# The second MLP product of a two-layer transformer kernel with seven block products instead of eight, on one Trainium2 core

## The chip, the core and the metric

The kernel runs on one core of a Trainium2 chip. A core has engines that run side by side, each with an instruction queue of its own: TensorE (PE in the profile; PEld are its weight loads), VectorE (DVE), ScalarE (ACT), GpSimd (POOL) and SyncE (SP), which here only issues DMA transfers. Transfers are issued from SP's queue and from ScalarE's (SPq and ACTq in the profile). Each engine takes its instructions in the order in which the program lists them, and an instruction waits on semaphores for those of other engines. TensorE multiplies from SBUF (128 partitions) into PSUM (eight banks of 2 KB a partition); the others read and clear PSUM. The metric is the time of one execution in microseconds, as the median of several runs.

## The reference

```python
def _A_ref(x, wqkv, wo):              # H = 32 heads of Dh = 20, window W = 256
    qkv = (x @ wqkv).reshape(B, S, 3, H, Dh).transpose(2, 0, 3, 1, 4)
    q, k, v = qkv[0], qkv[1], qkv[2]
    scores = jnp.einsum("bhqd,bhkd->bhqk", q, k) * (Dh ** -0.5)
    mask = (idx[:, None] - idx[None, :] >= 0) & (idx[:, None] - idx[None, :] < W)
    p = _softmax(jnp.where(mask[None, None], scores, -1e9))
    return jnp.einsum("bhqk,bhkd->bhqd", p, v).transpose(0, 2, 1, 3).reshape(B, S, D) @ wo

def _B_ref(x, w1, b1, w2, b2):        # D = 640, F = 1536
    h = jnp.einsum("bsd,df->bsf", x, w1) + b1
    r = jnp.where(h > 0, h, 0)
    return jnp.einsum("bsf,fd->bsd", r * r, w2) + b2

for _ in range(2):                    # x: 1 x 2048 x 640, the same weights in both layers
    x = x + _A_ref(_layernorm(x), wqkv, wo)
    x = x + _B_ref(_layernorm(x), w1, b1, w2, b2)
```

## The kernel before

**Numbers.** All is float32 in memory. Each large product is done with float16 halves: a matrix is split into a high part and the rest (low), and `mm3` (L256) issues three matmuls for each chunk of 128 rows of the contraction: high by high, high by low, low by high. The weights are converted once, at the start: `convert` (L196) writes the high half on ScalarE (L198) and the low half on VectorE (L199), and wq_s, wo_s, w1_s and w2_s then stay in SBUF for both layers. Weights on their way in are staged in memory that is free at that time: `load_wo` and `load_w1` stage in w2_s (L192), and `load_w2` in `krow[2]`, the memory of a later group's keys.

**Groups.** The 2048 tokens are worked through in 8 groups of T = 256, twice (two layers), so 16 units u. A unit's own attention runs beside the dense work of its neighbours, which stands in Python generators that yield after about 0.5 us of matmuls: `stage_qk(u + 1)` and `stage_v(u + 1)` (queries, keys and values of the next group), `stage_o(u - 1)` (output projection), `y_cross` (the second layernorm's result, transposed by DMA), and `stage_f(u - 1)` (the MLP). `together` (L930) deals these out between the eight quads of heads of the unit's attention. A quad is `max_quad` (scores for the row maxima: matmuls L548, VectorE L560), for every second quad `max_out` (transposes the maxima, L573, and puts them into the queries as two more rows by DMA), `exp_quad` (scores again, now less the maxima: matmuls L611, exponentials on ScalarE L624, and masks on GpSimd L639 and L643), and `pv_quad` (the values: float32 matmuls L673, which wait for the masks; ScalarE copies them out, L685). The output projection reads the values back through memory, transposed and divided by the sums of the exponentials (`load_o`; reciprocals L749).

**PSUM.** Two tiles of three banks hold scores (`banks`, name bb); the two banks that are left go in turn to all dense products, values and transposes (`mm_tile`, tag "mm").

**Order.** The program writes out the order of every engine's queue itself. Work for ScalarE ("A"), VectorE ("D"), GpSimd ("G") and DMA issue ("S") is posted as a Job with a cost in ns, a priority and the jobs that it depends on; a small clock for each engine (`pump`, `step`) places them as TensorE's planned time goes by, and `need` moves the planned time to the end of a job. So the order of a queue follows planned times, but on the chip each instruction just waits for its semaphores, in that order. FCST, CARRY and KEEP (L964) are planned costs of stages, by which `together` spreads the dense work.

**The MLP.** `stage_f` (L829) first does the first product, six times two chunks f of 128 hidden columns, 15 matmuls of 256 columns each: ScalarE adds b1 and takes relu (L844, out of PSUM into a float32 tile r), GpSimd squares (L848), ScalarE copies to the high half (L851), VectorE subtracts for the low half (L854), both into the tile hh. Then `ln_cross` posts the layernorm and the DMA transposes of the group after next. The second product takes two halves i of the tokens by two halves h of the 640 columns: 36 matmuls of 320 columns over 12 chunks, weights hh (loaded into TensorE), moving w2_s. VectorE adds each to the residual x1 (L881), to which GpSimd has added b2 (`add_b2`, L803), and x1 is stored (L890). The memory of hh (tag "hh") is also used by `stage_qk`, `y_cross` (through `beside`) and `load_o`.

## Time and profile before

| | before |
|---|---|
| median of 3 runs | 1628.66 us (1627.52 to 1630.12) |
| the profiled execution's span | 1624.5 us; the profile gives no time beside it |
| instructions in the span | 44743 |
| TensorE: idle before matmuls of the first MLP product | 4.5 us in the whole span |
| TensorE: idle before matmuls of the second MLP product | 0.0 us |
| mean rate of memory traffic | 85 GB/s read and written |

The profile is of one execution. Its page gives, for each engine, the busy time and its share of the span. The chain of waits follows the work that ended last back from the end: each row is a start, a length, an engine, and an instruction by its line with what it writes and reads. The instructions in order of time have the same columns for all work, with runs of equal instructions as one row (x35). A row of groups has busy time and mean ns of one behind the first bar, and the idle time of the engine just before these instructions, with what ended it, behind the second; "[7.81 <-ACT r L844]" is the same for one row. A row of a stretch has the length, then for PE, PEld, DVE, ACT and POOL the busy time with the count of instructions, then the clock granted to TensorE (1.00 is full), the share of time that the 16 DMA engines were busy, and GB/s. DMA issues have median issue, the range of their starts, and the median time to landing. "spin" are matmuls without use that the kernel issues at the start.

### The profile page before, as it was taken

The page shows a single profiled execution, that of the slowest core. Times are in us where ns is not written, and L with a number is a line of the kernel's source. Part 1 is how long each engine was busy: PE and PEld are TensorE (multiplying, and loading weights), DVE is VectorE, ACT ScalarE, POOL GpSimd, SP SyncE. Part 2 cuts the span into 40 slices and gives each one's busy share as a digit, 9 for nine tenths or more (in the row PEclk, how much of TensorE's full clock was granted, in tenths as well). Part 3 has the DMA queues.
Part 4 walks back from the last instruction along what each step waited for, and adds up shares of the span by engine and source line. Part 5 has one row for each costly group of instructions (what it writes and reads, how often), then busy time and mean ns, then how long its engine had stood idle before and what let it go on. Part 6 is the DMA issues. An engine that isn't in the chain of part 4 may idle for free.

```text
span 1624.5 us, 44743 instructions
## 1 busy us (share of the span) xinstructions
PE 1591.8 (98%) x17686; PEld 1181.1 (73%) x17686; DVE 1043.5 (64%) x3250; ACT 736.4 (45%) x1593; POOL 614.5 (38%) x1288
## 2 busy tenths in 40 slices
PE   8998999999999999999999999999999999999999
PEld 7676767777777777777777777777777777776667
DVE  8776775666756657665556766567675666757441
ACT  4555535444453444545344453534535444454522
POOL 1224524334352443535233352533534334343512
PEclk9999999999999999999999999999999999999999
DMA  9863253351434434343352434334343351431020
GB/s 272 204 173 93 59 127 75 109 113 50 115 83 116 90 73 113 70 119 79 94 132 58 119 77 121 80 94 107 67 115 79 106 112 50 108 75 54 26 65 17
DMA packets 234217, 158.09 MB, mean 97 GB/s; under 512 B 82200, under 2 KB 217752, under 8 KB 234008
## 3 DMA queue, kind: packets, MB, share of 16 engines
q1 hardware_dynamic: 227640, 145.74, 36.6%
q10 hardware_dynamic: 6368, 9.50, 1.9%
q8 instruction: 139, 2.28, 0.6%
q14 instruction: 70, 0.57, 0.1%
HBM read 84.68 MB, written 52.95 MB: 85 GB/s over the span
## 4 chain that ended last, share of the span: by engine, by line
PE 90%; DVE 4%; ACT 3%; DMA 1%; issue 1%; POOL 1%; SPq 0%; DVEq 0%; POOLq 0%; ACTq 0%
PE acc L261 67%; PE pv L673 10%; PE bb L611 6%; PE bb L548 5%; DVE bb L560 2%; ACT pt L624 1%; PE spin L275 1%; PE tr L573 1%; DMA o<-ot 0%; ACT r L844 0%; DMA od<-o 0%; DVE mx L560 0%; ACT qd L435 0%; DVE qd L438 0%; DVE mT L579 0%
## 5 line engine op out<-in xcount | busy, mean ns | idle before, releaser
L560 DVE CUSTOM_DVE_ANT_0 bb<-bb,maskb 128x384 f32<-128x384 f32 (+2 forms) x1024 | 510.6, 565 | 103.6 <-PE bb L548 95.9
L624 ACT ACTIVATE pt<-bb 128x512 f32<-128x512 f32 (+1 forms) x736 | 376.0, 600 | 235.8 <-PE bb L611 229.2
L639 POOL TENSOR_SCALAR_AFFINE_SELECT pt<-pt 128x256 f32<-128x256 f32 x448 | 198.8, 449 | 564.3 <-ACT pt L624 543.9
L261 PE MATMUL acc<-y,w_s 128*128 128x256 f16 x2880 | 330.4, 273 | 4.5 <-DVE y L311 1.4
L261 PE MATMUL acc<-w_s,hh 128*128 128x320 f16 x2304 | 326.7, 300 | 0.0
L261 PEld LDWEIGHTS <-w_s 128*128 128x128 f16 x2880 | 277.5, 98 | 58.0 <-issue 25.8
L261 PEld LDWEIGHTS <-hh 128*128 128x128 f16 x2304 | 222.0, 98 | 98.1 <-issue 15.3
L261 PEld LDWEIGHTS <-wq_s 128*128 128x128 f16 x2400 | 230.6, 98 | 47.0 <-issue 17.5
L261 PE MATMUL acc<-yT,wq_s 128*128 128x256 f16 x2250 | 258.9, 273 | 4.1 <-DMA yT<-yl 1.0
L643 POOL TENSOR_SCALAR_AFFINE_SELECT pt<-pt 128x256 f32<-128x256 f32 x512 | 220.1, 452 | 93.2 <-ACT pt L624 85.6
L854 DVE TENSOR_TENSOR hh<-r,hh 128x256 f16<-128x256 f32 x192 | 91.5, 498 | 204.7 <-ACT hh L851 197.1
L673 PE MATMUL pv<-pt,vt 128*32 128x128 f32 (+1 forms) x3840 | 187.5, 329 | 2.8 <-DVE x L783 1.7
L848 POOL TENSOR_TENSOR r<-r 128x256 f32<-128x256 f32 x192 | 113.8, 614 | 182.1 <-ACT r L844 180.6
L685 ACT COPY ot<-pv 128x256 f32<-128x256 f32 x128 | 47.7, 372 | 283.9 <-PE pv L673 283.8
L560 DVE DVE_READ_ACCUMULATOR2_ANT mx<- 128x1 f32 x1024 | 143.2, 140 | 0.0
L261 PE MATMUL acc<-wo_s,od 128*128 128x320 f16 x960 | 139.6, 301 | 0.0
L673 PEld LDWEIGHTS pv<-pt,vt 128*32 128x32 f32 x3840 | 104.0, 109 | 48.6 <-issue 18.2
L261 PE MATMUL acc<-wq_s,yT 128*128 128x320 f16 x900 | 132.2, 299 | 3.6 <-DVE y L311 1.9
L844 ACT ACTIVATE r<-acc,b1s 128x256 f32<-128x256 f32 x192 | 80.7, 472 | 98.5 <-PE acc L261 97.0
L261 PEld LDWEIGHTS <-od 128*128 128x128 f16 x960 | 92.0, 98 | 43.4 <-issue 8.7
L261 PEld LDWEIGHTS <-yT 128*128 128x128 f16 x900 | 86.6, 98 | 41.2 <-issue 10.7
L611 PE MATMUL bb<-qt,kt 62*128 62x128 f16 (+1 forms) x1920 | 107.1, 244 | 4.1 <-DVE mx L560 3.0
(82 smaller groups left out, 1182.7 us busy)
## 6 DMA issues: line engine op xcount, KB each, us to landing
qt<-qk SPq DMA_DIRECT2D x30, 480.0 KB
kt<-qk SPq DMA_DIRECT2D x30, 480.0 KB
qk<-qd SPq DMA_DIRECT2D x17, 640.0 KB
o<-ot SPq DMA_DIRECT2D x256, 42.0 KB
od<-o SPq DMA_DIRECT2D x14, 640.0 KB
qk<-yl SPq DMA_DIRECT2D x13, 640.0 KB
qk<-qd SPq DMA_DIRECT2D x17, 320.0 KB
xt<-in_A_x_dram SPq DMA_DIRECT2D x16, 320.0 KB
```

What stands on the lines that cost most here:

```text
L261: nc.tensor.matmul(acc, lhs(a, c), rhs(b, c), start=(k == 0), stop=(k == 3 * nk - 1))
L548: nc.tensor.matmul(to, qt[r, p, i * P:(i + 1) * P], kt[r, p, a:b], start=True, stop=True)
L560: nc.vector.tensor_tensor_reduce(out=v, in0=v, in1=mask, scale=1.0, scalar=-3.0e38, op0=ALU.add, op1=ALU.max, accum_out=accum),
L611: nc.tensor.matmul(bb[e][:, k, o:o + w], kt[r, 2 * qd + j, ko:ko + P], qt[r, 2 * qd + j, q0 * P:q0 * P + w], start=True, stop=True)
L624: nc.scalar.activation(box["pt"][:, :o], bb[e][:, k, :o], AF.Exp, scale=SCALE / (QS * QS))
L639: nc.gpsimd.affine_select(out=m, in_=m, pattern=[[0, 2], [-1, P]], compare_op=ALU.is_gt, fill=0.0, base=0, channel_multiplier=1)
L643: nc.gpsimd.affine_select(out=m, in_=m, pattern=[[0, 2], [1, P]], compare_op=ALU.is_ge, fill=0.0, base=0, channel_multiplier=-1)
L673: nc.tensor.matmul(pv[32 * jj:32 * (jj + 1), q0 * P:(q0 + qn) * P], vf[:, c:c + 32], pj[:, j, :], start=(k == 0), stop=(k == len(steps) - ...
L685: nc.scalar.copy(ot[:, qd % 2], pv)
L844: nc.scalar.activation(box["r"], acc[:, f, :], AF.Relu, bias=b1s[:, f0 + f:f0 + f + 1], scale=1.0 / (YS * WS))
L848: nc.gpsimd.tensor_tensor(box["r"], box["r"], box["r"], op=ALU.mult)
L854: nc.vector.tensor_sub(hh[:, 1, f, :], box["r"], hh[:, 0, f, :])
```

## The change

The second product Y = A B (A: 256 tokens by 1536 hidden columns, squared; B: w2) is cut once in each of its three dimensions: tokens into halves i, hidden columns into halves k (chunk p goes with chunk p + 6, a pair), columns into halves h. With A11, A12, A21, A22 (first index the token half) and B likewise, Winograd's form of Strassen's method computes seven products of sums instead of eight:

- on the left: A11, A12, S1 = A21 + A22, S2 = S1 - A11, S4 = A12 - S2, S3 = A11 - A21, A22, of which the tile r holds some with the other sign; the weights' signs go with them;
- on the right: the seven matching blocks or sums of blocks of w2;
- the four outputs as sums of the products. Products are numbered j = 0 to 6, and one of them goes into one or two of the outputs x1 (list ADDS).

What it does to the code, with line numbers of the changed kernel where the prediction uses them:

- **First product's evictions** now run by pairs p of chunks, six a group, in a tile r of eight blocks of 128 columns (two such tiles instead of four of 256 columns): per chunk relu on ScalarE and square on GpSimd as before, then on GpSimd three instructions for the sums (128, 256 and 128 columns), one copy of 896 columns to the high half (ScalarE, L937) and one subtraction of 896 columns for the low half (VectorE, L941). The halves go into two tiles (tags "ha" and "hb").
- **Second product**: 7 products x 6 pairs x 3 = 126 matmuls of 320 columns in 21 pieces (two pairs of a product each), in the order PIECES. Products 0, 2, 4 and 5 add up one after the other in one PSUM bank, "x": VectorE reads it after each, and the next starts only after the reads. Products 1, 3 and 6 use the other bank, "y", each by itself. There are eight adds into x1 on VectorE (L993) instead of four. The two banks stay open over several pieces, so `some` and `together` hold back attention's use of the "mm" banks while they are open.
- **Weights**: the sums of w2's blocks are formed at the start on GpSimd, split into halves on ScalarE and VectorE, and written to device memory (w2d, 6 x 1.15 MB), staged through the ring's memory. `fetch` then reads pieces of 327,680 B back into a ring of seven places, from ScalarE's DMA queue, one for every piece of every group (336 in all). Each waits for the matmuls that free its place, and for the fetch eight transfers before it. w2_s is gone; `load_w1` and `load_wo` stage in other memory. The first seven fetches stand behind the first group's attention; group 0's first product waits for the weight sums, since they use the same tiles r.
- **Planned costs**: FCST, CARRY and KEEP are changed.

```diff
+FP = FC // 2
+SLOTS = 7
...
-    w2_s = sb.tile([P, 2, FC, D], F16, name="w2_s")
+    ring = sb.tile([P, SLOTS, 2, 2, HD], F16, name="ring")
+    w2d = tc.dram_tile([P, 7, FC // 2, 2, HD], F16, name="w2d")
...
     def load_w2():
...
+
+        v = w2.rearrange("(k c p) n -> c p k n", p=P, c=FP)
+        places = [hraw2[:, :2 * D], hraw2[:, 2 * D:4 * D], krow[2][:, :2 * D]]
+        outs = [ringraw[:, k * 7 * HD:(k + 1) * 7 * HD].bitcast(F16).rearrange("p (j a n) -> p j a n", a=2, n=HD)
+                for k in range(2)]
+        lows, done = {}, {}
+        for p in range(FP):
+            st, out = places[p % 3], outs[p % 2]
+            free = lows[p - 3] if p > 2 else [[*w1s[1]], [*w1s[2]], [gate2]][p]
+            load = bulk(lambda st=st, p=p: nc.scalar.dma_start(st.rearrange("p (k n) -> p k n", k=2), v[p]),
+                        P * 2 * D * 4, gate, *free)
+            q = st.rearrange("p (k n) -> p k n", n=HD)
+            box = {}
+
+            def sums(box=box, q=q):
+                box["t"] = t = sb.tile([P, 8, P], F32, name="r", tag="r", bufs=2)
+                t = t.rearrange("p a n -> p (a n)")[:, :3 * HD].rearrange("p (a n) -> p a n", n=HD)
+                box["t"] = t
+                nc.gpsimd.tensor_tensor(t[:, 1:3], q[:, 1:2].to_broadcast([P, 2, HD]), q[:, 0::3], op=ALU.subtract)
+
+            def more(box=box, q=q):
+                nc.gpsimd.tensor_tensor(box["t"][:, 0], q[:, 3], box["t"][:, 1], op=ALU.subtract)
+
+            def last(box=box, q=q):
+                t = sb.tile([P, 8, P], F32, name="r", tag="r", bufs=2)
+                box["l"] = t = t.rearrange("p a n -> p (a n)")[:, :HD]
+                nc.gpsimd.tensor_tensor(t, q[:, 2], box["t"][:, 0], op=ALU.subtract)
+
+            j = post("G", 1600, sums, load, *(lows.get(p - 1, ())), prio=2)
+            j = post("G", 850, more, j, prio=2)
+            j = post("G", 850, last, j, prio=2)
+            kinds = [(lambda q=q: q[:, 0::2], slice(0, 2), WS, 2, load), (lambda box=box: box["t"], slice(2, 5), WS, 3, j),
+                     (lambda box=box: box["l"], 5, WS, 1, j), (lambda q=q: q[:, 3], 6, -WS, 1, load)]
+            lows[p] = []
+            for src, at, s, n, d in kinds:
...
+                a = post("A", 60 + 0.85 * n * HD, high, d, *done.get(p - 2, ()), *(w1j.values() if p < 2 else ()), prio=2)
+                lows[p].append(post("D", 60 + 1.1 * n * HD, low, a, prio=2))
+            done[p] = [bulk(lambda out=out, p=p: nc.scalar.dma_start(w2d[:, :, p], out), P * 14 * HD * 2, *lows[p])]
+        w2l.extend(j for k in range(FP) for j in lows[k])
+        w2j.extend(j for k in range(FP) for j in done[k])
...
+    PIECES = [("x", 0, 0), ("x", 0, 1), ("y", 1, 0), ("y", 1, 1), ("x", 0, 2), ("y", 1, 2)] + [
+        (b, j, g) for b, j in (("x", 2), ("y", 3), ("x", 4), ("y", 6), ("x", 5)) for g in range(3)]
+    PLACE = [0, 1, 4, 6, 5, 2, 3]
+    slots = {}
+
+    def fetch(n, *deps):
+
+        _, j, g = PIECES[n % len(PIECES)]
+        if n < len(PIECES) * NU:
+            slots[n] = post("A", 150.0, lambda: nc.scalar.dma_start(ring[:, n % SLOTS], w2d[:, j, 2 * g:2 * g + 2]), *deps,
+                            prio=1, size=P * 4 * HD * 2, land=2200.0)
...
+            sides[u] = sb.tile([P, 2, KC * 2 * T], F16, name="yl", tag="hb", bufs=1)
...
+            raw = sb.tile([P, 2, KC, T], F32, name="od", tag="ha", bufs=1)
...
     def stage_f(u, ahead=None):
...
+        if u == 0:
+            need(*w2l)
+        hs = [sb.tile([P, 2, FP // 2, 7, P], F16, name="hh", tag=t, bufs=1) for t in ("ha", "hb")]
         hj = []
...
+        for p in range(FP):
             acc, jobs = mm_tile([P, 2, T], "acc")
...
+            def evict(wait, acc=acc, jobs=jobs, p=p):
+                box, js = {}, []
+                for k in range(2):
+                    def blocks(box=box, k=k):
+                        return box["r"][:, 1:3] if k else box["r"][:, 0::7]
+
+                    def relu(k=k, acc=acc, box=box, blocks=blocks):
+                        if k == 0:
+                            box["r"] = sb.tile([P, 8, P], F32, name="r", tag="r", bufs=2)
+                        f = p + k * FP
+                        nc.scalar.activation(blocks(), acc[:, k, :].rearrange("p (i n) -> p i n", i=2), AF.Relu,
+                                             bias=b1s[:, f:f + 1], scale=1.0 / (YS * WS))
+
+                    def square(blocks=blocks):
+                        nc.gpsimd.tensor_tensor(blocks(), blocks(), blocks(), op=ALU.mult)
+
+                    j = post("A", 360, relu, *hj[max(p - 2, 0):max(p - 1, 0)], *jobs[-1:], wait=wait, prio=0)
                     jobs.append(j)
...
+                    js.append(post("G", 571, square, j, prio=0))
+
+                def s1(box=box):
+                    r = box["r"]
+                    nc.gpsimd.tensor_tensor(r[:, 6], r[:, 7], r[:, 2], op=ALU.add)
+
+                def s23(box=box):
+                    r = box["r"]
+                    nc.gpsimd.tensor_tensor(r[:, 4:6], r[:, 6:8], r[:, 0:1].to_broadcast([P, 2, P]), op=ALU.subtract)
+
+                def s4(box=box):
+                    r = box["r"]
+                    nc.gpsimd.tensor_tensor(r[:, 3], r[:, 4], r[:, 1], op=ALU.subtract)
+
+                def high(box=box):
+                    nc.scalar.copy(hs[p // 3][:, 0, p % 3], box["r"][:, 0:7])
+
+                def low(box=box):
+                    h = hs[p // 3]
+                    nc.vector.tensor_sub(h[:, 1, p % 3], box["r"][:, 0:7], h[:, 0, p % 3])
+
+                j = post("G", 330, s1, *js, prio=0)
+                j = post("G", 571, s23, j, prio=0)
+                j = post("G", 330, s4, j, prio=0)
+                j = post("A", 830, high, j, prio=0)
+                hj.append(post("D", 1060, low, j, prio=0))
+
+            for k in range(2):
+                fo = (p + k * FP) * P
+                need(w1j[p + k * FP])
+                yield from mm3(acc[:, k, :], lambda a, c: w1_s[:, a, c, fo:fo + P],
+                               lambda b, c: y2[:, b, c, :], KC, 109, evict if k else None)
         if ahead is not None:
             ln_cross(ahead, *b2j)
...
+        x1 = [x1s.pop((u, i)) for i in range(2)]
+        ADDS = [[(0, 0)], [(0, 0)], [(0, 1)], [(1, 1), (0, 1)], [(1, 1)], [(1, 0)], [(0, 1)]]
+        LAST = {1: [(0, 0)], 6: [(0, 1)], 4: [(1, 1)], 5: [(1, 0)]}
+        reads = []
+        started = set()
+        for n, (bank, j, g) in enumerate(PIECES):
+            n += u * len(PIECES)
+            if opened[bank] is None:
                 acc, jobs = mm_tile([P, 2 * T], "acc")
...
+                hold = Job("S", 0.0, None, [], 0.0, 0)
+                jobs.append(hold)
+                opened[bank] = acc, jobs, hold
+                started.discard(bank)
+            acc, jobs, hold = opened[bank]
+            if bank == "x" and g == 0 and reads:
+                need(*reads)
+            need(slots[n])
+            for c in range(2):
+                p = 2 * g + c
+                need(hj[p])
+                for k, (a, b) in enumerate(((0, 0), (0, 1), (1, 0))):
+                    nc.tensor.matmul(acc[:, :HD], hs[p // 3][:, a, p % 3, PLACE[j], :], ring[:, n % SLOTS, c, b, :],
+                                     start=bank not in started, stop=(p == FP - 1 and k == 2), skip_group_check=True)
+                    started.add(bank)
+                if c == 0:
+                    yield 408
+            used_ = Job("S", 0.0, None, [], 0.0, 0)
+            used_.end = now[0] + 408
+            fetch(n + SLOTS, used_)
+            if g < 2:
+                yield 408
+                continue
+            js = []
+            for i, h in ADDS[j]:
+                hs_ = slice(h * HD, (h + 1) * HD)
+
+                def add(x=x1[i], acc=acc, hs_=hs_):
+                    nc.vector.scalar_tensor_tensor(x[:, hs_], acc[:, :HD], 1.0 / WS, x[:, hs_], op0=ALU.mult, op1=ALU.add)
+
+                js.append(post("D", 408, add, *b2j[2 * i + h:2 * i + h + 1], wait=408, prio=0))
+            jobs.extend(js)
+            if bank == "x":
+                reads = js
+            if bank == "y" or j == 5:
+                jobs.remove(hold)
+                opened[bank] = None
+            for i, h in LAST.get(j, ()):
+                b, hs_ = 2 * g_(u) + i, slice(h * HD, (h + 1) * HD)
                 if u == NU - 1:
...
+                    dma(lambda x=x1[i], b=b, hs_=hs_: nc.sync.dma_start(out_rows[b * P:(b + 1) * P, hs_], x[:, hs_]),
+                        P * HD * 4, js[-1], prio=0)
+                elif (i, h) in ((0, 1), (1, 0)):
+                    stored.append(dma(lambda x=x1[i], b=b: nc.sync.dma_start(
+                        xs[b] if l + 1 < NL else out_rows[b * P:(b + 1) * P, :], x), P * D * 4, js[-1]))
+                    waiting.pop(len(stored) - 1, lambda: None)()
+            yield 408
...
     def some(dense, cost):
 
-        while cost > 0 or not all(banks2):
+        while cost > 0 or not all(banks2) or opened["x"]:
...
+            while opened["y"]:
+                c = next(dense)
+                step(c)
+                done += c
...
-    QKC, VC, OC, FCST, LNC, CARRY, KEEP, MID = 16.4e3, 8.2e3, 8.2e3, 39.2e3, 1.2e3, 15e3, 20e3, 8e3
+    QKC, VC, OC, FCST, LNC, CARRY, KEEP, MID = 16.4e3, 8.2e3, 8.2e3, 36.8e3, 1.2e3, 25e3, 27e3, 8e3
...
+    for n in range(SLOTS):
+        fetch(n, *w2j)
```

83 lines of the change are left out of this document (23 added, 60 removed).

## The prediction

> **What bounds the kernel now.** I read the page first, then the chain that ended last, then the instructions in order of time for one group of 256 tokens, and last the busy times of its two MLP stages.
>
> ```profile
> span 1624.5 us, 44743 instructions
> PE 1591.8 (98%) x17686; PEld 1181.1 (73%) x17686; DVE 1043.5 (64%) x3250; ACT 736.4 (45%) x1593; POOL 614.5 (38%) x1288
> ```
>
> TensorE is busy all along, but a busy PE may be pipelined matmuls, so the chain and the timeline have to say whether it waits. In the chain the same piece of work comes back once per group:
>
> ```profile
> 309.97 5.57 PE acc L261 x50
> ...
> 408.44 5.57 PE acc L261 x50
> ```
>
> A group takes 408.44 - 309.97 = 98.47 us. In the group that runs its MLP at 1034 us, TensorE does this (columns: start, length, instruction):
>
> ```profile
> 1034.28 3.98 PE L261 MATMUL acc<-y,w_s 128*128 128x256 f16 x35
> 1038.19 0.83 PE L611 MATMUL bb<-qt,kt 62*128 62x256 f16 x16
> 1038.96 5.09 PE L261 MATMUL acc<-y,w_s 128*128 128x256 f16 x45
> 1043.97 0.84 PE L548 MATMUL bb<-kt,qt 60*128 60x128 f16 x18
> 1044.74 1.51 PE L673 MATMUL pv<-pt,vt 128*32 128x256 f32 x32
> 1046.18 3.99 PE L261 MATMUL acc<-y,w_s 128*128 128x256 f16 x35
> ...
> 1060.69 2.34 PE L261 MATMUL acc<-w_s,hh 128*128 128x320 f16 x16
> ...
> 1063.73 5.06 PE L261 MATMUL acc<-w_s,hh 128*128 128x320 f16 x36
> 1068.72 0.84 PE L548 MATMUL bb<-kt,qt 60*128 60x128 f16 x18
> ...
> 1086.82 0.83 PE L611 MATMUL bb<-qt,kt 62*128 62x256 f16 x16
> ```
>
> Each row starts as the last one ends, none has an idle time behind it. So the first MLP product (I call it F1, from 1034.28) and the second (W2, 1060.69 to 1086.82) stand on TensorE's own rate, and the 52.54 us of both are its work. From start to start, a matmul of F1 is (1043.97 - 1038.96)/45 = 0.111 us, one of W2 (1068.72 - 1063.73)/36 = 0.139 us, the scores of a quad (L611) or its maxima (L548) 0.77 us, its values (L673) 1.44 us. The other engines have room, by stage (columns: PE, PEld, DVE, ACT, POOL busy, clock, DMA share, GB/s):
>
> ```profile
> 1034.28:1060.69 26.41, 26.27 (x313) 21.28 (x313) 14.19 (x47) 14.88 (x35) 15.70 (x30) 1.00 0.31 64
> 1060.69:1086.82 26.13, 26.13 (x280) 17.71 (x278) 18.03 (x59) 9.89 (x20) 8.44 (x20) 1.00 0.33 74
> ```
>
> GpSimd is the one to watch: 15.70 of 26.41 us in F1.
>
> **What is removed.** W2 goes from 4 x 36 = 144 matmuls to 7 x 18 = 126 a group: 18 x 0.139 = 2.50 us, over 16 groups 40.0 us. That is the whole gain, and all of it lies on the path.
>
> **What is added to a pair of chunks.** F1 is now evicted six times a group, by pairs. GpSimd squares twice and then forms sums of 128, 256 and 128 columns; the copy to high halves and the subtraction for low halves take 896 columns at once.
>
> ```profile
> 1037.75 0.84 ACT L844 ACTIVATE r<-acc,b1s 128x256 f32<-128x256 f32 x2 [3.00 <-PE acc L261]
> 1039.84 2.05 ACT L624 ACTIVATE pt<-bb 128x512 f32<-128x512 f32 x4
> ...
> 1038.31 1.19 POOL L848 TENSOR_TENSOR r<-r 128x256 f32<-128x256 f32 x2 [7.81 <-ACT r L844]
> ...
> 1029.36 1.13 POOL L643 TENSOR_SCALAR_AFFINE_SELECT pt<-pt 128x256 f32<-128x256 f32 x3
> 1045.42 3.33 POOL L803 TENSOR_TENSOR x<-x,xt 128x320 f32<-128x320 f32 x4
> ...
> L851 ACT CAST hh<-r 128x256 f16<-128x256 f32 x192 | 74.1, 411 | 38.2 <-POOL r L848 37.8
> L372 ACT CAST yl<-xt 128x640 f16<-128x640 f32 x52 | 37.8, 735 | 51.8 <-DVE xt L300 49.6 <-PE acc L261 1.8 <-ACT pt L624 0.5
> L854 DVE TENSOR_TENSOR hh<-r,hh 128x256 f16<-128x256 f32 x192 | 91.5, 498 | 204.7 <-ACT hh L851 197.1
> L376 DVE TENSOR_TENSOR yl<-xt,yl 128x640 f16<-128x640 f32 x52 | 41.8, 821 | 4.8 <-ACT yl L372 4.8
> L881 DVE SCALAR_TENSOR_TENSOR x<-acc,x 128x320 f32<-128x320 f32 x60 | 29.5, 492 | 81.4 <-PE acc L261 81.3
> ```
>
> The sums have two different operands, as the bias adds of L803: 3.33/4/320 = 2.6 ns a column, so 0.33 + 0.67 + 0.33 = 1.33 us; with the squares (1.19) a pair is 2.52 us. A high copy of 896 columns, on the line through 411 and 735 ns, is 0.95 us; a low one, on that through 498 and 821, about 1.1. The chain of a pair with nothing in its way: 0.56 us until the squares start (1037.75 to 1038.31), 1.19, 1.33, 0.95, 1.1 = 5.1 us. Before, the chain had no sums and ran in chunks of 256 columns.
>
> GpSimd's F1 stage grows by 6 x 1.33 = 8.0 us to 23.7 of some 26: nearly full. Its queue is served in order, and that costs TensorE twice. I follow the order in which the changed kernel's instructions stand, with t = 0 at F1's first matmul.
>
> *First stall, in pair 2.* TensorE does 20 matmuls, scores (0.77), 10, pair 1's 30, 5 of pair 2, maxima (0.77), and stands at the values of that quad at 65 x 0.111 + 2 x 0.77 = 8.8. They need masks on exponentials that ScalarE, with six of them (2.05/4 each) and an eviction (0.84) from 3.0 on, has done by 6.9. But on GpSimd the quad's last two masks stand behind all of pair 1's work. Pair 0 ends on TensorE at 30 x 0.111 + 0.77 = 4.1; its sums end at 4.1 + 0.56 + 1.19 + 1.33 = 7.2; its high copy stands in front of pair 1's evictions on ScalarE, until 8.1; pair 1's GpSimd work then starts at 8.6 and, with one mask between, ends at 8.6 + 2.52 + 0.38 = 11.5; two masks (1.13/3 each) end at 12.2. The last third of the values (0.48) ends at 12.7 where it would have been 10.2: about 2.4 us lost. What is late next is pair 2 and the adds of b2, which hide it. Bounds: 0 (exponentials and pair 1 earlier than I have them) and 2.4 with another us of queueing, 3.4.
>
> *Second stall, at the last pair.* After F1's last matmul come scores (0.77), 24 matmuls of W2 on finished pairs, and three on pair 4: 0.77 + 27 x 0.139 = 4.5 us, then the last pair is needed. Its bare chain is 5.1 us, so 0.6 us is lost at least. In its way stand pair 4's high copy before its evictions (about 0.6 left of 0.95), a mask (0.38) and a fetch (below, 0.34): 6.4 us, a loss of 1.9. The upper bound adds another 1 us: 2.9.
>
> I take both as worked out: 4.3 us a group against 2.50 gained, net +1.8; bounds 0.6 - 2.5 = -1.9 and 6.3 - 2.5 = +3.8.
>
> **The ring.** 21 fetches a group are put in ScalarE's queue, each of 327,680 B, and wait for the matmuls that free their place.
>
> ```profile
> L248 ACTq DMA_DIRECT2D kt<-in_B_w_dram x12: 334/341/445, 86.7 to 148.8; - x12
> ...
> q10 hardware_dynamic: 432, 0.98, 14.6%
> ```
>
> The loads of w2 have the same form: 341 ns of issue, and in the stretch of 20 us (140 to 160 us) of the second row three of them took 0.146 x 20 = 2.92 us of all engines, 0.97 each. The issues are 7.2 us in a stage in which ScalarE is busy 9.89 of 26.13: hidden; queued behind them are exponentials, whose scores stand behind the same pieces on TensorE. A piece is used in (26.13 - 2.5)/21 = 1.13 us; seven are there at the start, so the 14th fetch is due 20 pieces in, at 22.5 us. With the share of 0.33 that other transfers have, a fetch takes 0.97/0.67 = 1.45: the 14th lands about 1.1 + 14 x 1.45 = 21.4. Taken as nothing; if the queues halve each other it is the second rival.
>
> The Trainium skill (DMA: Bandwidth & Descriptors, Queues, rings and completion order) says that a DMA engine takes turns between the queues that have work, packet by packet. By that rule a fetch beside a busy SP queue takes twice as long; no row of before has such a meeting long enough to show it.
>
> **Adds and bank changes.** Eight adds a group instead of four are 4 x 0.492 = 2 us more of VectorE, of 18.03 busy in 26.13: hidden, except where the next user of the bank follows at once, after 0.8 us of scores or maxima. Taken as 0, at most 0.7 a group. While bank y is open no quad of attention starts; this moves quads by a product at most and costs nothing by itself. The copies that start the next group's transposes stand behind fetches now:
>
> ```profile
> 1079.23 1.22 SPq L379 DMA_TRANSPOSE yT<-yl x1
> ```
>
> The last one was issued 7.6 us before W2's end; in the new order it stands behind the maximum rows of the same quad and comes some 4 us before it. Taken as 0, at most 1.
>
> **Start.** w2 is now converted with sums, staged through the ring, written out (6.9 MB) and read back; F1 of group 0 has the same buffers.
>
> ```profile
> 110.09 2.70 DVE L199 SCALAR_TENSOR_TENSOR w_s<-kt,w_s 128x640 f16<-128x640 f32 x3
> 112.71 0.95 DVE L749 RECIPROCAL rs<-rs 128x64 f32<-128x64 f32 x2
> ...
> 147.65 1.25 PE L261 MATMUL acc<-y,w_s 128*128 128x256 f16 x10
> ```
>
> Ahead of the reciprocals that free the first output projection stand 3200 columns of conversion instead of 1920: at 2.70/1920 that is 1.8 us late. GpSimd's sums are 6 x 1280 x 2.6 ns = 20 us, a conversion's 2240 columns of low halves at 2.70/1920 are 3.2 us behind 3.3 of sums, with the first high copy about 7 us; six in a row from 110 us end near 152, where F1 began at 147.65: 4 us. Sum +6, between 0 (the spins before the projection hide it) and 15 (another 1.5 us for each conversion).
>
> **End.** The last two groups run without attention beside W2:
>
> ```profile
> 1601.47 19.72 PE L261 MATMUL acc<-w_s,hh 128*128 128x320 f16 x144
> ```
>
> Each gains 2.5 and loses the 1.9 of the last pair: together -1.
>
> **Sum.** 13 groups x 1.8 = 23, + 6 - 1 = +28. The profiled span becomes 1652.5; the runs shown have a median of 1628.66, 4.2 us over the span, so 1656.7, which I round to 1657. Own range: 13 x (1.0 to 3.0) with the start 0 to 15, 1641 to 1682.
>
> **Rivals.**
>
> *The chains are met in time (faster).* If exponentials and pair 1 come early enough that the masks are through at 8.8, only the bare 0.6 us is lost: 14 x (0.6 - 2.5) = -27, start +6, end -2: 1606. For it: in before nothing waits, and GpSimd's 23.7 still fit. Against it: the order on GpSimd's queue is fixed. It decides from the point where the stalls of a group are under 2.5 us.
>
> *The stream is late (slower).* At 1.94 us a fetch the 14th lands at 28.3, 5.8 us late, in each of 13 groups; with half of the stage so shared, some 2.4 us: +31, 1688. For it: the DMA share of 0.33 in W2, and the transposes and loads of the next group in it. Against: ring and deadline fit at the mean.
>
> *The clock falls in the new gaps (slower).*
>
> ```profile
> 1.43 6.13 PE spin L275 x28
> ...
> 109.96 9.20 PE L275 MATMUL spin<-ident 128*128 128x128 f32 x80
> ...
> 120.00:128.00 8.00, 6.34 (x81) 4.29 (x80) 4.63 (x16) 0.75 (x2) 0.00 (x0) 1.00 1.00 239
> ```
>
> At the start a spin takes 0.219 us, later 0.115, so TensorE has a slower gear, which the clock column doesn't tell. After the 1.66 us idle at 120 to 128 us the values still took their usual time. If gaps of 2.4 us bring it, 6.13 us at the slow rate lose 2.9: 13 x 2.9 = +38, 1695. The Trainium skill (TensorE: Matmul & The Clock Gate, Part 1: The HAM clock gate) has the clock halved after an idle window of about 3.4 us; by that rule neither gap alone is long enough.
>
> **How the numbers follow.** The chain case 0.55; late stream 0.11; clock 0.04; chains met 0.22; the rest, 0.08, lies between the chain case and the faster one, 0.05 of it within 0.2%. The time is 1657. The range 1608 to 1690 takes in the edge of the faster case and the late stream. About 0.2% is what a measurement tells from no change: faster 0.25, same 0.05, slower 0.70.
>
> **What would show it.** Right: a group of about 100.3 us between equal pieces of the chain; TensorE idle before the values in F1, released by GpSimd's masks, and idle in W2 before the last pair, released by VectorE's L941; GpSimd busy some 23 of 28 us in F1. Wrong: a group near 96 us and no such idle; or the longest waits on fetches of the ring.

## The result and the profile after

The changed kernel takes 1973.97 us (median, 1967.99 to 1978.56), before 1628.09 us in the same comparison: a ratio of 1.2122, 95% interval 1.2098 to 1.2145. It is 346 us slower. The profiled execution, beside a span of 1624.5 us before, has these rows on its page and in its chain of waits:

```profile
span 1976.8 us, 44962 instructions
PE 1700.5 (86%) x17398; PEld 1203.1 (61%) x17398; DVE 1106.3 (56%) x3230; ACT 757.8 (38%) x1509; POOL 832.0 (42%) x1594
...
1080.98 7.79 PE acc L323 x44
...
1200.37 7.98 PE acc L323 x45
```

TensorE issues 288 matmuls fewer, and is now idle for 276 us of the span (33 before). From one of these pieces to the other are 1200.37 - 1080.98 = 119.4 us, a group, 20.9 more than before. Laid out by first matmuls of the first product F1: up to that of the second group 308.6 us (before 256.6), then twelve groups in 1445.0 (1176.7), then 223.2 to the end (191.2): 52 + 268 + 32 = 352 us of span. The last of the twelve alone takes 145.4 us (103.6), with waits of 9.48 and 2.39 us for the last group's keys; the other eleven take 118.1 on average (97.6). In order of time, TensorE in the group whose F1 starts at 1130.30, with the idle time before a row in brackets:

```profile
1138.36 0.84 PE L610 MATMUL bb<-kt,qt 60*128 60x128 f16 x18
1140.07 1.03 PE L735 MATMUL pv<-pt,vt 128*32 128x256 f32 x18 [0.88 <-POOL pt L701]
1142.35 0.42 PE L735 MATMUL pv<-pt,vt 128*32 128x128 f32 x6 [1.25 <-POOL pt L705]
1143.94 0.99 PE L735 MATMUL pv<-pt,vt 128*32 128x256 f32 x8 [1.17 <-POOL pt L705]
1144.86 5.62 PE L323 MATMUL acc<-y,w_s 128*128 128x256 f16 x35
...
1158.85 1.34 PE L735 MATMUL pv<-pt,vt 128*32 128x128 f32 x16 [0.94 <-POOL pt L701]
1160.85 0.63 PE L735 MATMUL pv<-pt,vt 128*32 128x256 f32 x6 [0.66 <-POOL pt L705]
...
1166.12 3.84 PE L977 MATMUL acc<-ring,hh 128*128 128x320 f16 x27
1172.07 0.70 PE L977 MATMUL acc<-ring,hh 128*128 128x320 f16 x2 [2.11 <-ACT hh L937]
1173.48 2.05 PE L977 MATMUL acc<-ring,hh 128*128 128x320 f16 x7 [0.71 <-DVE hh L941]
1175.46 1.46 PE L610 MATMUL bb<-kt,qt 60*128 60x128 f16 x18
1176.86 2.51 PE L735 MATMUL pv<-pt,vt 128*32 128x256 f32 x32
...
1192.31 1.51 PE L735 MATMUL pv<-pt,vt 128*32 128x256 f32 x32 [0.81 <-DVE x L993]
...
1200.37 7.98 PE L323 MATMUL acc<-yT,wq_s 128*128 128x256 f16 x45 [3.18 <-DMA yT<-yl]
```

Three things happen here. The values of both quads in F1 wait for masks, and the last pair is late in the second product W2: the two places that were predicted, and one more, F1's second quad. The next group's first matmul waits for its transposes, for which nothing was put into the sum. And several rows take twice their time: 35 matmuls 5.62 us instead of 4.00, 32 of the values 2.51 instead of 1.51, 45 behind the transposes 7.98 instead of 5.09. The stretches show why (after the five busy times the granted clock, the DMA share, GB/s):

```profile
1130.30:1166.12 35.82, 30.92 (x331) 22.89 (x328) 15.24 (x44) 15.29 (x30) 26.42 (x45) 0.95 0.28 62
1166.12:1197.20 31.08, 27.16 (x261) 17.21 (x259) 19.87 (x56) 10.48 (x20) 11.14 (x23) 0.89 0.77 204
...
1140.00:1142.00 2.00, 1.03 (x18) 0.67 (x18) 2.00 (x8) 0.00 (x0) 1.92 (x4) 1.00 0.00 0
1142.00:1144.00 2.00, 0.48 (x7) 0.21 (x8) 1.47 (x6) 0.45 (x1) 1.92 (x5) 1.00 0.00 0
1144.00:1146.00 2.00, 2.00 (x14) 1.04 (x15) 1.47 (x2) 0.87 (x2) 2.00 (x3) 0.71 0.02 4
1146.00:1148.00 2.00, 2.00 (x11) 1.38 (x10) 1.07 (x5) 0.00 (x0) 2.00 (x3) 0.50 0.02 4
1148.00:1150.00 2.00, 2.00 (x20) 1.72 (x18) 0.00 (x0) 0.57 (x2) 0.39 (x2) 0.94 0.00 0
```

GpSimd is busy 26.42 us in F1, as long as F1 took before (26.41). Of F1's 9.4 us more, 0.77 are the 16 scores of one quad (L673), which the new order moves there out of W2. In W2 the DMA share is 0.77 instead of 0.33. And behind a stretch of waits the clock stands at half rate for 0.29 x 2 / 0.5 + 2 + 0.06 x 2 / 0.5 = 3.4 us. GpSimd's groups in the changed kernel (behind the bar busy time and mean ns):

```profile
L918 POOL TENSOR_TENSOR r<-r 128x256 f32<-128x256 f32 x192 | 132.6, 710 | 101.5 <-ACT r L914 99.8
L930 POOL TENSOR_TENSOR r<-r 128x256 f32<-128x256 f32 x96 | 70.8, 738 | 6.6
L926 POOL TENSOR_TENSOR r<-r 128x128 f32<-128x128 f32 x96 | 45.4, 473 | 7.4
L934 POOL TENSOR_TENSOR r<-r 128x128 f32<-128x128 f32 x96 | 44.2, 460 | 6.4
```

A pair costs 2 x 0.710 + 0.738 + 0.473 + 0.460 = 3.09 us, not 2.52. The transposes' way, on SP's queue, ScalarE's and VectorE's:

```profile
1172.05 3.85 ACTq L311 DMA_DIRECT2D ring<-w2d  x3
1175.94 0.73 ACT L434 CAST yl<-xt 128x640 f16<-128x640 f32 x1 [3.42 <-DMA ring<-w2d]
...
1176.69 8.12 SPq L441 DMA_TRANSPOSE yT<-yl  x2
...
1190.94 0.83 DVE L438 TENSOR_TENSOR yl<-xt,yl 128x640 f16<-128x640 f32 x1 [2.35 <-ACT yl L434]
...
1192.92 2.63 SPq L441 DMA_TRANSPOSE yT<-yl  x2
...
1192.92 7.40 DMA yT<-yl
```

The last row is of the chain: from issue to landing. The copy that starts a transpose stands on ScalarE behind fetches that wait, the second subtraction comes 24.8 us after W2's first matmul, and the last two transposes are issued from 1192.92, 4.3 us before TensorE is ready for the next group (1200.37 - 3.18 = 1197.19). That is the lead that was foreseen; but they take 7.40 us to land. Before, the last one went out 8.4 us ahead of the next group's first matmul (the prediction's 7.6 goes to the last scores in front of it).

### The profile page after: what moved, and what is told of

Read it like the earlier page. It is cut to its first block, busy times and chain, and to the rows that moved or that the text cites. A ratio compares the mean times of both kernels' runs of the same rounds, so it can differ in the third digit from the quotient of the medians.

```text
span 1976.8 us, 44962 instructions
## 1 busy us (share of the span) xinstructions
PE 1700.5 (86%) x17398; PEld 1203.1 (61%) x17398; DVE 1106.3 (56%) x3230; ACT 757.8 (38%) x1509; POOL 832.0 (42%) x1594
## 3 DMA queue, kind: packets, MB, share of 16 engines
q1 hardware_dynamic: 227640, 145.74, 31.6%
q10 hardware_dynamic: 60128, 126.51, 21.6%
## 5 line engine op out<-in xcount | busy, mean ns | idle before, releaser
L686 ACT ACTIVATE pt<-bb 128x512 f32<-128x512 f32 x736 | 377.5, 599 | 352.0 <-PE bb L673 247.2
L323 PE MATMUL acc<-y,w_s 128*128 128x256 f16 x2880 | 358.5, 288 | 12.7 <-ACT r L914 10.8
L977 PE MATMUL acc<-ring,hh 128*128 128x320 f16 x2016 | 304.6, 308 | 45.5 <-ACT hh L937 21.1
L323 PE MATMUL acc<-yT,wq_s 128*128 128x256 f16 x2250 | 290.9, 290 | 50.7 <-DMA yT<-yl 46.8
L735 PE MATMUL pv<-pt,vt 128*32 128x128 f32 (+1 forms) x3840 | 229.3, 348 | 74.3 <-POOL pt L705 41.2
L977 PEld LDWEIGHTS <-hh 128*128 128x128 f16 x2016 | 194.7, 100 | 149.6 <-issue 28.9
L941 DVE TENSOR_TENSOR hh<-r,hh 128x896 f16<-128x896 f32 x96 | 114.9, 1197 | 304.1 <-ACT hh L937 304.1
L937 ACT CAST hh<-r 128x896 f16<-128x896 f32 x96 | 90.1, 938 | 179.5 <-POOL r L934 170.3
L360 POOL TENSOR_TENSOR bmv<-bmv,neghalf 128x1 f32<-128x1 f32 x64 | 42.7, 668 | 260.4 <-DVE bmv L354 260.3
L673 PE MATMUL bb<-qt,kt 62*128 62x128 f16 (+1 forms) x1920 | 115.9, 246 | 36.5 <-DVE mx L622 16.8
L610 PE MATMUL bb<-kt,qt 60*128 60x128 f16 (+1 forms) x2176 | 113.6, 245 | 27.0 <-ACT pt L686 15.1
```

The lines of the kernel that those rows point to most:

```text
L323: nc.tensor.matmul(acc, lhs(a, c), rhs(b, c), start=(k == 0), stop=(k == 3 * nk - 1))
L610: nc.tensor.matmul(to, qt[r, p, i * P:(i + 1) * P], kt[r, p, a:b], start=True, stop=True)
L673: nc.tensor.matmul(bb[e][:, k, o:o + w], kt[r, 2 * qd + j, ko:ko + P], qt[r, 2 * qd + j, q0 * P:q0 * P + w], start=True, stop=True)
L686: nc.scalar.activation(box["pt"][:, :o], bb[e][:, k, :o], AF.Exp, scale=SCALE / (QS * QS))
L735: nc.tensor.matmul(pv[32 * jj:32 * (jj + 1), q0 * P:(q0 + qn) * P], vf[:, c:c + 32], pj[:, j, :], start=(k == 0), stop=(k == len(steps) - ...
L937: nc.scalar.copy(hs[p // 3][:, 0, p % 3], box["r"][:, 0:7])
```

## The experiments

The columns are one group of each kernel, the tenth: from start to start of TensorE's first matmuls, first part of the next group's queries and values (QV1), output projection (O), their second part (QV2), F1, and W2 up to the next QV1, so with the wait for the transposes. "Mean" is the mean of twelve groups, from the F1 of the second to that of the fourteenth.

| kernel | us | QV1 | O | QV2 | F1 | W2 | mean |
|---|---|---|---|---|---|---|---|
| before | 1628 | 15.6 | 11.3 | 18.3 | 26.4 | 26.9 | 98.1 |
| changed | 1974 | 18.5 | 12.1 | 19.0 | 35.8 | 34.7 | 120.4 |
| sums on VectorE | 2013 | 23.3 | 12.1 | 19.0 | 37.1 | 34.7 | 124.5 |
| no fetches | 1881 | 15.6 | 12.1 | 19.0 | 36.5 | 30.5 | 113.5 |
| both of these | 1901 | 21.0 | 12.1 | 19.0 | 36.9 | 26.4 | 116.0 |
| spins | 1993 | 15.6 | 12.1 | 19.0 | 36.3 | 34.4 | 120.0 |
| fewer spins | 1938 | 17.0 | 12.1 | 19.0 | 34.5 | 34.3 | 116.5 |
| no sums | 1891 | 24.9 | 12.1 | 19.0 | 29.5 | 31.6 | 114.9 |
| costs, early b2 | 1921 | 20.9 | 12.1 | 19.0 | 32.6 | 30.3 | 116.5 |
| small fetches | 1893 | 15.6 | 12.1 | 19.0 | 37.2 | 28.4 | 113.4 |
| CARRY, KEEP of before | 1959 | 18.3 | 12.1 | 19.0 | 35.8 | 34.6 | 118.0 |
| last fetches in O | 2026 | 15.6 | 21.4 | 19.0 | 36.5 | 31.1 | 124.1 |
| last three together | 1995 | 15.6 | 24.2 | 19.0 | 34.3 | 29.9 | 122.0 |
| the same, half the squares on ScalarE | 1983 | 15.6 | 23.8 | 19.0 | 33.1 | 33.1 | 121.1 |
| last fetches in F1 | 1884 | 15.7 | 12.1 | 19.0 | 36.5 | 30.5 | 113.4 |
| neither sums nor fetches | 1770 | 21.6 | 12.1 | 19.0 | 29.5 | 24.7 | 105.6 |
| mended | 1750 | 15.7 | 12.1 | 19.0 | 29.1 | 27.5 | 103.5 |
| neither, layernorm first | 1770 | 15.6 | 12.1 | 19.0 | 29.5 | 30.1 | 105.3 |
| mended, layernorm first | 1788 | 15.6 | 12.1 | 19.0 | 29.1 | 32.5 | 106.8 |

Each was timed beside before (1625 to 1631 us). The last one was executed four times: its ratio to before is 1.0975 (1.0953 to 1.0996). All others are single executions; the changed kernel's own four spread over 11 us, so differences of that size between two rows say nothing. Kernels without sums or fetches, or with small ones, and "spins" compute other numbers and tell only of times.

O and QV2, which the change doesn't touch, are 0.8 and 0.7 us longer in every variant (O but for the late fetches). Part of it is that scores wait there for row maxima, 0.25 us at a time; the rest was not traced.

### The sums: on VectorE, and left out

```diff
-  nc.gpsimd.tensor_tensor(r[:, 6], r[:, 7], r[:, 2], op=ALU.add)
...
-  j = post("G", 330, s1, *js, prio=0)
+  nc.vector.tensor_tensor(r[:, 6], r[:, 7], r[:, 2], op=ALU.add)
...
+  j = post("D", 230, s1, *js, prio=0)
```

> The three sums of a pair (128, 256, 128 columns) go from GpSimd to VectorE; all else as in the changed kernel, same result. My theory now: a group lost 21 us, of which about 9 in the first product (values of both its quads wait for masks that stand behind squares and sums on GpSimd, and the matmuls after the longer wait run at half rate), about 6 before the last pair of the second, about 7 at the transposes of the next group. Without the sums GpSimd has 1.7 us less a pair; the 9 go and 1 of the 6: 10 us a group, about 1835 us. Rival (ScalarE's queue or the two tiles r, not GpSimd, set the pace of the pairs): VectorE's sums take as long a place in the chain, within 30 us of 1974. Rival (the fetches are the cause of nearly all): no change.

F1 became 37.1 us. TensorE's rows in order of time say that the wait moved:

```profile
1292.29 0.32 PE L673 MATMUL bb<-qt,kt 62*128 62x256 f16 x1 [3.01 <-DVE mx L622]
...
1308.81 0.27 PE L673 MATMUL bb<-qt,kt 62*128 62x256 f16 x1 [2.44 <-DVE mx L622]
```

The values no longer wait, but the next scores wait for row maxima, which now stand behind sums on VectorE. That neither confirms nor refutes GpSimd's part, so the sums were taken away (two fixed tiles r in place of the rotating ones; jobs s1, s23 and s4 dropped):

> The three sums of each pair are left out and go to no engine (their blocks keep old contents, so the second product is made of wrong numbers); copies and subtractions of 896 columns stay. Since the sums on VectorE only moved the wait (scores waited for row maxima there), this asks GpSimd's theory purely: GpSimd's work in the first product falls from 26.4 to some 17 us, the values no longer wait, the first product takes about 27 us, the last pair comes 1.7 us earlier: 119.4 - 9 - 3 = 107 us a group, about 1805 us. Rival (two tiles r and ScalarE's order set the pace of the pairs): the first product stays over 33 us and the time over 1930.

F1 came down by 6.3 us to 29.5, and the last pair was in time. What is left over before's 26.4 are 0.8 us of the scores that moved, 1.7 us of waits for ScalarE's exponentials, whose queue also holds the copies of 896 columns, and 0.6 us more. One of the waits:

```profile
1214.21 0.21 PE L619 MATMUL bb<-kt,qt 60*128 60x128 f16 x1 [0.87 <-ACT pt L695]
```

But QV1 grew to 24.9 us, so only 83 us of the expected 169 came back.

### The fetches: left out, made small, moved

```diff
-  if n < len(PIECES) * NU:
+  if n < SLOTS:
```

> Only the first seven pieces of weights are fetched; the other 329 fetches are left out, so the second product uses wrong weights after the seventh piece. My theory: the transposes of the next group come in time again and the slow matmuls behind them go, about 7 us a group, and something at the start of the group's attention; first product unchanged at 35 to 37 us. About 1870 us. Rival (late pieces and traffic are the main cost): the group comes to near 100 us, total under 1720. Rival (the transposes are late because of VectorE's order, not of fetches): over 1950.

QV1 is 15.6 us again, W2 4 us shorter, F1 unchanged within 0.7: 93 us of the 104 expected. Sums on VectorE and no fetches together gave less, 1901 us:

> Sums on VectorE and only the first seven fetches (wrong weights after them). If the two causes add up, 1835 + 1870 - 1974 = about 1730; if the clock penalty joins them (one stall makes the next one longer), lower, under 1700; if what is left is neither (start, end, last pair), what remains over 1606 shows there.

With all fetches issued but 32 B each:

> All 336 fetches are issued with their waits, but after the first seven each moves 32 B a partition instead of 2560 B (wrong weights). If what makes the transposes late is the traffic and the landing of fetches: as without fetches, about 1880. If it is ScalarE's queue, which stands at fetches until TensorE frees their places: near 1974. I expect the first, with perhaps 10 us over it.

1893 us: it is the bytes and when they land, not the wait for a free place, which these fetches keep. Seven of the 21 fetches of a group are for the next one. They were first moved to the output projection:

```diff
+  if n % len(PIECES) < len(PIECES) - SLOTS:
       fetch(n + SLOTS, used_)
+  else:
+      kept.append((n + SLOTS, used_))
...
   def stage_o(u):
+      while kept:
+          fetch(*kept.pop(0))
```

> Result unchanged; the last seven fetches of a group, which are for the next one, are issued at the beginning of the output projection instead of during the second product. If the transposes are late because these last fetches stand in their way (in ScalarE's queue, on the shared completion semaphores, in the traffic), the time from the first matmul of the second product to that of the next group comes to about 30.5 us as without any fetches, and the matmuls behind it to 15.6 us: 6 us a group, about 1895 us. Rival (the first fourteen fetches alone are enough to make them late): over 1940.

The transposes were in time, but O took 21.4 us. ScalarE's queue and TensorE there, in order of time:

```profile
1245.08 8.44 ACTq L311 DMA_DIRECT2D ring<-w2d  x6
...
1254.70 4.69 PE L323 MATMUL acc<-wo_s,od 128*128 128x320 f16 x17 [5.71 <-ACT ot L747]
```

Six issues in a row took 8.44 us. Most of it is the last one's wait, 5.1 us, which ends when a load of queries from SP's queue (qt<-qk) lands; the copy that frees TensorE's bank stood behind them. Spread over F1, from SP's queue, the same seven cost nothing there:

> Result unchanged. The last seven fetches of a group go out during the next group's first product, one for each pair and two for the first, from SP's queue instead of ScalarE's; the first fourteen stay. If the run with late fetches lost in the output projection only because seven issues in a row held up ScalarE's queue, that projection comes back to 12.1 us, the gain around the transposes stays (30.4 and 15.6 us), 6 us a group: about 1895 us. Rival (the seven fetches cost about the same wherever they go): over 1950.

1884 us, as without any fetches: of the stream, these seven were the loss. Place and queue were changed together, so this doesn't tell which of the two helped. What it mended, the traces tell. SP's queue and TensorE in this run, in the same group as above:

```profile
1130.27 2.53 SPq L441 DMA_TRANSPOSE yT<-yl  x2
...
1133.96 5.22 PE L323 MATMUL acc<-yT,wq_s 128*128 128x256 f16 x45
```

The last two transposes are issued 3.7 us before the next group's first matmul, no earlier than in the changed kernel (4.3), and TensorE doesn't wait for them. So these fetches made the transposes late mostly by their time to land: 7.40 us there, at most 3.7 here.

### The clock

> Matmuls without use fill the places where TensorE waits: 5 ahead of each third of the values in the first product (into columns of the bank that nobody reads), 15 ahead of the last pair, 25 ahead of the next group's first product; result unchanged. The waits themselves stay. Theory that the clock's half rate after a wait costs some 7 us a group: granted clock near 1.00 in these places and 14 x 6 = 85 us less, about 1890. Rival (slow matmuls are an effect of late data, not of the clock): 1974 or more, as the spins lengthen what they fill.

1993 us, 19 more than the changed kernel. In this trial the spins began a new accumulation in banks that were being summed up, which changes the numbers that come out. The clock stayed at 1.00 in F1 and QV1 was 15.6, but the 30 instructions ahead of a pair and the 50 ahead of QV1 took longer than the gaps.

> As the run with spins, but about half as many, and none ahead of the first third: 3 ahead of the second and third thirds of the values, 7 ahead of the last pair, 12 ahead of the next group's first product (a spin is two instructions of 0.13 us, so the first trial filled more than the gaps). If the clock's half rate costs time of its own: under 1950, with the 45 matmuls behind the transposes at 5.0 us instead of 7.8. Rival: the penalty in the first product and before the last pair is covered by GpSimd's chain, which goes on meanwhile; then only the some 3 us a group behind the transposes come back, 1935 to 1950; if not even these, 1974 or more.

1938 us, and 3.9 us a group less: at least that much is the half clock and no late data. F1 gained 1.3 of it.

### The planner's costs, and the parts together

> Result unchanged. The planner is given the measured costs on GpSimd (square 640, sums 530, 800 and 530 ns instead of 571, 330, 571 and 330; copy 900), and the adds of b2 are posted before the values of the next group instead of inside the first product, so that GpSimd has 3.4 to 4.2 us less there. If GpSimd is simply overfull in the first product (26.4 us busy), it gets 4 to 5 us shorter: about 1915 us. If the order on its queue is the cause, the new order alone may give more, down to 1880. Rival (GpSimd isn't the cause): 1974 within 20.

F1 became 1.5 to 3 us shorter and W2 4 us, and QV1 gave back 2: 52 us in all. The new costs and the early adds were not tried apart.

> Result unchanged; of the change only the planned costs CARRY and KEEP go back from 25 and 27 to 15 and 20 us. From the last full group on (1677.8 us) the changed kernel takes 299.0 us where before took 241.5 (1383.0 to 1624.5). If the larger CARRY causes it by drawing the last group's attention ahead of its keys (TensorE waited 9.48 + 2.39 us for them, and 0.3 to 3 us at many scores), this comes down to about 270 us and the time to 1945. Rival (the tail has the same causes as a group): within 8 us of 1974.

15 us, half of the expected 29. Gone is the wait for the last group's keys, in the changed kernel on TensorE:

```profile
1745.24 0.26 PE L610 MATMUL bb<-kt,qt 60*128 60x128 f16 x1 [9.48 <-DMA kt<-qk]
```

The next two have the late fetches at the place that blocked ScalarE, and so they lose in O (1995 and 1983 us):

> Result unchanged; measured costs and early adds of b2, CARRY and KEEP of before, and late last fetches together. If the parts add up: 1921 - 6 x 13 - 30 = about 1815. If the stalls that are left become longer as others go (as without the sums, where the transposes then waited), 1850 to 1880.

> As the run with all of these, and one of a pair's two squares is done by ScalarE instead of GpSimd (3.6 us less on GpSimd a group, 2.5 us more on ScalarE). If GpSimd's queue is what the values wait for, the first product comes from 33 to about 29 us, and the time is 40 us under that run; if ScalarE's order takes over, within 10 us of it.

Half the squares on ScalarE took 1.2 us off F1, not 4. With the fetches' place in F1 instead, and the masks at the pairs' priority:

> Result unchanged; all that helped together: measured costs on GpSimd and early adds of b2, one of two squares on ScalarE, CARRY and KEEP of before, last fetches in the next first product from SP, and the masks with the same priority as the pairs' work. First product about 30 us, second with the transposes 29, projection 12.1: about 107 us a group and 1790 us in all. Rival (the wait moves again, to ScalarE or to the pairs): 1850 or more.

1750 us and 103.5 a group, 224 us better than the changed kernel; still 124 us slower than before beside it. The granted clock is 1.00 in both stages (rows of stretches):

```profile
1114.10:1143.20 29.10, 27.45 (x332) 21.96 (x330) 14.59 (x44) 17.29 (x36) 21.35 (x39) 1.00 0.57 147
1143.20:1170.60 27.40, 24.31 (x261) 15.88 (x259) 19.44 (x56) 10.39 (x20) 10.62 (x22) 1.00 0.82 197
```

### A third cause in a group

> No sums on GpSimd, only the first seven fetches, CARRY and KEEP of before (wrong numbers in the second product). If sums and fetches are the whole loss of a group, a group takes 98.5 - 2.5 + 1 for bank changes, 97 us, and with start and end as they are (some 50 and 30 us late) the time is about 1690 us. If a third cause is hidden behind these two (the copies of 896 columns, two tiles r, attention's new places), 102 us a group or more, over 1750.

105.6 us a group, not 97. W2 is 24.7 us, 2.2 below before: 18 matmuls less (2.50) and the scores that moved to F1 (0.77) would be 3.3, and 0.7 are waits. But QV1, 6.1 us longer than before, waits for transposes. VectorE's and SP's rows:

```profile
1181.12 0.57 DVE L631 CUSTOM_DVE_ANT_0 bb<-bb,maskb 128x384 f32<-128x384 f32 x1 [0.38 <-PE bb L619]
...
1185.61 0.81 DVE L447 TENSOR_TENSOR yl<-xt,yl 128x640 f16<-128x640 f32 x1
...
1186.65 1.23 SPq L450 DMA_TRANSPOSE yT<-yl  x1
```

The subtraction stands behind the eight maxima of W2's second quad, and the last transpose goes out when W2 (from 1161.5) is over.

```diff
-  ln_load(u, *deps)
+  ln_load(u, *deps, prio=0)
...
-  ... sb.tile([P, 2, 2, D], F16, name="yl", tag="qd", bufs=1))
+  ... sb.tile([P, 2, 2, D], F16, name="yl", tag="qd", bufs=1), 0)
```

> As the run with neither sums nor fetches (wrong numbers in the second product), and the next group's layernorm and its two copies have the first priority in the queues. If the place on VectorE's queue is the third cause, the next group's first product starts without a wait and takes 15.6 us instead of 21 to 23: about 101.5 us a group, some 1700 us. Rival (adds into x1 and bank changes hold the layernorm up whatever its place): over 1755.

Half right: QV1 is 15.6 us, and W2 30.1. Now an add into x1 stands behind the layernorm, and the values wait for its bank:

```profile
1175.86 0.48 DVE L999 SCALAR_TENSOR_TENSOR x<-acc,x 128x320 f32<-128x320 f32 x1
...
1176.49 2.61 PE L744 MATMUL pv<-pt,vt 128*32 128x256 f32 x32 [3.98 <-DVE x L999]
```

So the third cause is VectorE's order in W2: with the bank to be read after each product, layernorm, adds and maxima compete for the same moment. It is most of what is left, not all: F1 (29.5), O and QV2 are longer than before in these runs too. That an order exists in which neither waits long was seen in the mended version (QV1 15.7, W2 27.5), and the same priority there spoils it:

> As the mended run, with the layernorm's jobs first; result unchanged. There the transposes were already in time, so the same group of 103 us, 1750 us; it stays slower than before whatever the order, since the start (34.5 us late at the second group's first product) and the end (25 us) are still there and a group has not come under 98.5.

It costs 39 us over the mended version. What a group of that would need to come under 98.1, and the later start, were not tried further: before stays the fastest of all.

## Why the prediction was wrong

The sign was right, the size was not: 1657 us and at most 1690 against 1974. Three steps fail: terms that were put at next to nothing (transposes, clock), waits of F1's second quad that were taken as hidden, and a start and an end that were costed by lengths of queues or not at all. By its steps:

| step | predicted | measured |
|---|---|---|
| a group, net | +1.8 | +20.6 (eleven groups), +41.8 the twelfth |
| removed matmuls, a group | -2.50 | -2.2 (W2 with neither sums nor fetches, its 0.7 of waits and the 0.77 of moved scores taken out) |
| GpSimd's work on a pair | 2.52 | 3.09 |
| values in F1 | 2.4, 0 to 3.4, one quad | waits of 3.3 and 1.6, two quads; F1 +9.4 with the clock and 0.77 of moved scores |
| last pair | 1.9, 0.6 to 2.9 | 2.8, and 2.7 more at half clock |
| bank changes | 0, at most 0.7 | 0.81 |
| transposes | 0, at most 1 | 3.2, and 2.9 more at half clock |
| start | +6, 0 to 15 | +52 |
| end | -1 | +32, and the twelfth group's wait for keys |

- **First stall.** The mechanism was right, with the masks behind pair 1's work, and its 3.3 us lie within the bounds. What failed is "What is late next is pair 2 and the adds of b2, which hide it". GpSimd was full, not nearly full: a short instruction costs more than the line through 320 columns gave (0.46 us instead of 0.33 for 128), so the second quad of F1 met the same queue.
- **Second stall.** Right in place and cause, and at the upper bound in size; with the sums left out it is gone. What was missing is the clock behind it: 7 matmuls, maxima and values take from 1173.48 to 1179.37, 5.9 us for 7 x 0.139 + 0.77 + 1.44 = 3.2.
- **"Taken as 0, at most 1"** for the copies that start the transposes is the step that failed outright. I had seen that they stand behind maxima and come some 4 us before W2's end, and that came true (4.3). What I left out is the time from issue to landing, 7.40 us beside the fetches: 7.40 - 4.3 = 3.1 of the wait of 3.2. The lateness has two causes that the runs told apart: the seven fetches for the next group, by the time to land, and VectorE's order, which without sums and fetches put the last issue behind W2's end.
- **"The ring. Taken as nothing."** The deadline of the pieces held, as worked out: what the stream made late was its neighbours. The rule of the Trainium skill (DMA: Bandwidth & Descriptors, Queues, rings and completion order), by which a DMA engine takes turns between queues, would by my estimate have doubled a fetch's time; no run here separates turns of packets from mere bytes.
- **The clock** was given 0.04, on the ground that no gap was long enough. It fell behind waits of 0.88, 1.25 and 1.17 us with matmuls between them, and was back after some 3.4 us. In the 4 us to 1144.0 TensorE had worked 1.03 + 0.48 us. Over the whole trace of the changed kernel the granted clock falls 54 times: in the 3.4 us before each TensorE was busy for at most 58%, and before half of them no single idle time was longer than 1.4 us. The rule of the Trainium skill (TensorE: Matmul & The Clock Gate, Part 1: The HAM clock gate) that I read as a need for an idle window does not agree with this. The length of the slow stretch, 3.4 us, agrees with the window of that section.
- **The rivals** were priced as alternatives, each with a chance of its own. Late masks, late transposes and the slow clock were all true in the same group, and a mean of exclusive cases can't reach that. But even all upper bounds together, 13 x (3.8 + 0.7 + 1 + 2.9) + 15 + 31 for the late stream = 155 us, stay far under 346. The range was narrower still: it took 1.0 to 3.0 us a group, without a reason, where the two stalls had been worked out as -1.9 to +3.8.
- **Start and end.** At the start the lengths of queues were costed, but not what waits on what: two waits alone, one for an eviction that itself waits for the last conversion of weight sums (ACT L914, released by VectorE's L292) and one for the second group's transposes, are 19.9 us. Near the end no row was costed for CARRY, which accounts for 15 us (the run with the old values). What else makes up the 52 and 32 us was not tried apart.

The two largest waits of the start, on TensorE:

```profile
178.38 5.86 PE L323 MATMUL acc<-y,w_s 128*128 128x256 f16 x35 [9.44 <-ACT r L914]
...
260.18 6.90 PE L323 MATMUL acc<-yT,wq_s 128*128 128x256 f16 x44 [10.49 <-DMA yT<-yl]
```

## What to carry to other kernels

In a kernel whose TensorE is full, saved matmuls are worth their time only if no other engine comes near full in the same stage: look at the busy time of each engine in that stage against the stage's new, shorter length, and ask what stands behind each added instruction in its queue. A stream of transfers is to be costed by whom it makes wait, not only by its own deadline, and what isn't needed in this stage goes to one in which the DMA engines have room (F1 here, with a share of 0.28 against 0.77 in W2). A transfer that someone waits for is to be costed up to its landing, beside the traffic of that moment. Stalls don't exclude each other: add them, and add what the clock takes after them.

## What the runs showed of the hardware

TensorE's clock halves without a long idle time (above), so a stall of 3.3 us in three pieces cost 1.6 us more. And VectorE's subtractions with two operands in SBUF hold up GpSimd. Rows of both engines in the changed kernel:

```profile
1154.05 1.09 DVE L941 TENSOR_TENSOR hh<-r,hh 128x896 f16<-128x896 f32 x1 [1.96 <-ACT hh L937]
...
1154.08 1.33 POOL L705 TENSOR_SCALAR_AFFINE_SELECT pt<-pt 128x256 f32<-128x256 f32 x1
1158.39 0.41 POOL L701 TENSOR_SCALAR_AFFINE_SELECT pt<-pt 128x256 f32<-128x256 f32 x1
```

A mask that takes 0.41 us alone took 1.33 beside the subtraction of 1.09. Over the whole trace the 108 masks that overlap such a subtraction take 0.76 us on average, the 551 that overlap no `tensor_tensor` or `scalar_tensor_tensor` of VectorE 0.42. This agrees with the Trainium skill (GPSIMD Engine Reference, Key points), by which GpSimd shares its SBUF interfaces with VectorE and is hindered by its instructions with two SBUF inputs. Before, beside subtractions of 256 columns, no mask took more than 0.79 us: one instruction of 896 columns is a longer block.
